# Centred rows by row tile at the head of a GLU + attention kernel, with the first weights loaded earlier

## The chip, the cores and the metric

The kernel runs on one core of one Trainium2 chip. The metric is the device time of one execution in microseconds (us). An execution also has a *span*, from the first to the last instruction in its trace; here the time is nearly always 1.7 to 2.0 us above the span.

## The reference, cut to what matters

```python
xn = _layernorm(x)                                   # (x - mean) / sqrt(var + 1e-5), 2048 rows of 512
s  = attention(xn @ wq, k_cache, v_cache) @ wo       # 32 heads, 2048 keys, Dh = 128
gate = xn @ W_gate; up = xn @ W_up                   # 512 -> 1792
h = relu(gate) * up
g = silu(h @ W_down)
return x + s * g
```

The change rests on one identity. With the centred row `xc = x - mean` and `r = 1/sqrt(var + eps) > 0`, `gate = r * (xc @ W_gate)` and `up = r * (xc @ W_up)`. ReLU passes a positive factor through, so `h @ W_down = r^2 * (h_c @ W_down)`. Gate and up can therefore run on centred rows before `r` is known, if `r^2` is applied at the SiLU.

## The kernel before

The kernel computes the GLU first and the attention after it. The GLU's gate and up use a ring of three slots of two PSUM banks (one for gate, one for up); a slot comes free when ReLU (ACT) and the product (DVE) have read it. The first 512 rows need special care, because nothing is in SBUF yet.

```python
load_x0(sp, 0); load_x0(act, 1); load_x0(sp, 2); load_x0(act, 3)   # 128 rows each
load_w(sp, Wg_sb, wg_src, sem_wg, 0); load_w(sp, Wu_sb, wu_src, sem_wu, 0)   # chunks 0 to 2
# ... later weights and rows ...

def ring_acquire():
    s = ring_cnt[0] % NSLOT
    ring_cnt[0] += 1
    _wait_all(pe, ring_tok[s])          # [ReLU token, product token] of the last user
    ring_tok[s] = []
    return s

def head_ln():
    st = ln_stats(0)
    st = ln_stats(1)
    sq01 = ln_aggr([0, 1], st)          # aggregate, then Sqrt on ACT
    st = ln_stats(2)
    c01 = ln_coef([0, 1], sq01)         # reciprocal, -mean*rstd
    n0 = ln_norm(dve, sem_ln4, 0, c01)
    n1 = ln_norm(dve, sem_ln4, 1, c01)
    head_transpose(0, n0, act, sem_xa)  # 4 PE transposes, ACT copy to xnT
    head_transpose(1, n1, act, sem_xa)
    warm_mm(3)
    # ... tiles 2 and 3 alike ...
    emit_half(0, range(HFC - 1), xt_ready[0][0:2])   # 256 columns at a time, chunks 0 and 1
    # ... then chunk 2, then emit_half(1, ...) for the other 256 columns

_wait(pe, warm_w)
warm_mm(12)                             # 512-column matmuls on zeros
head_ln()
```

After the head, `emit_gate_up` runs the remaining eleven chunks of the first 512 rows with 512-column ("full-width") matmuls. The first of these takes slot 0, so it waits until ReLU and product of chunk 0 are done.

The softmax here doesn't subtract the row's maximum and nothing guards it: scores larger than these inputs give would overflow.

## Time and profile before

| what | value |
|---|---|
| time | 1288.09 us, median of 3 (1287.98 to 1288.51) |
| span of the profiled execution | 1285.8 us |
| first useful matmul | 7.80 us |
| first full-width matmul | 13.48 us |

The page first: busy time of each engine, and the shares of the chain of work that ended last.

```profile
PE 1279.2 (99%) x11995; PEld 834.8 (65%) x11995; DVE 380.0 (30%) x682; ACT 1001.4 (78%) x1109; POOL 10.0 (1%) x21
...
PE 99%; DVE 1%; issue 0%; DMA 0%; ACT 0%
```

TensorE (PE) bounds the kernel. What is left to win is what lies in front of its first useful work. The waits of PE in the first 140 us (engine, line, what it waited for; total us, times, longest) are three:

```profile
PE ps_r L365 <- DVE warm L235: 1.2, 1, 1.2
PE ps_acc L353 <- DVE xn_sb L340: 0.7, 1, 0.7
PE ps_r L407 <- ACT xnT L359: 0.4, 1, 0.4
```

The chain of waits of the same kernel in its first 16 us, each piece with start and length in us:

```profile
0.74 2.39 DMA x_sb<-in_A_x_dram
...
3.15 1.30 DVE stats L315 x2
...
4.47 0.25 DVE mv L320 x2
...
5.40 0.17 DVE nmr L334
...
5.60 0.42 DVE xn_sb L340
...
6.16 0.40 PE ps_acc L353 x4
...
6.58 1.08 ACT xnT L359 x2
...
7.80 1.91 PE ps_r L407 x16
```

And the first full-width matmul of before, in the timeline of PE:

```profile
13.48 1.03 PE L481 MATMUL ps_r<-xnT,Wg_sb 128*128 128x512 bf16 x4
```

Two tiles go through the whole layer norm and two copies before PE can start at 7.80. From there PE is busy to the end, apart from a wait of 0.4 us near the last instruction.

### The profile page before, as it was taken

How to read it: one execution, taken by the hardware profiler on the slowest of the kernel's cores; microseconds unless marked ns; L12 is line 12 of the kernel's file. 1: busy time of each engine (PE TensorE's matmuls, PEld its weight loads, DVE VectorE, ACT ScalarE, POOL GpSimd, SP SyncE). 2: the span in 40 equal slices, each digit the busy share in tenths (PEclk: the TensorE clock that was granted, in tenths of full speed). 3: DMA queues.
4: the chain of work that ended last, by engine and by line, in shares of the span. 5: the costliest groups of instructions: out<-in, count | busy, mean ns of one | idle time of the engine just before them, and what ended most of it. 6: DMA issues, size and time to landing. Idle time of an engine off the chain costs nothing.

```text
span 1285.8 us, 26847 instructions
## 1 busy us (share of the span) xinstructions
PE 1279.2 (99%) x11995; PEld 834.8 (65%) x11995; DVE 380.0 (30%) x682; ACT 1001.4 (78%) x1109; POOL 10.0 (1%) x21
## 2 busy tenths in 40 slices
PE   9999999999999999999999999999999999999998
PEld 4444476666666666666666666666666666666665
DVE  6333311112222222222222222222222222234456
ACT  3322399998888888888888888888888888888884
POOL 2000000000000000000000000000000000000000
PEclk9999999999999999999999999999999999999999
DMA  9500123232222332232322322332223321233302
GB/s 266 111 1 1 21 36 67 57 54 40 36 51 50 71 54 50 54 71 51 54 46 37 60 47 53 55 67 55 54 51 71 55 34 38 50 67 55 50 14 74
DMA packets 238801, 71.60 MB, mean 56 GB/s; under 512 B 225632, under 2 KB 238688, under 8 KB 238688
## 3 DMA queue, kind: packets, MB, share of 16 engines
q1 hardware_dynamic: 238400, 69.63, 27.8%
q8 instruction: 96, 1.57, 0.5%
q10 hardware_dynamic: 288, 0.26, 0.1%
q14 instruction: 17, 0.14, 0.0%
HBM read 32.77 MB, written 2.10 MB: 27 GB/s over the span
## 4 chain that ended last, share of the span: by engine, by line
PE 99%; DVE 1%; issue 0%; DMA 0%; ACT 0%
PE ps_acc L722 36%; PE ps_r L625 34%; PE ps_r L558 9%; PE ps_r L579 8%; PE ps_acc L504 4%; PE ps_r L485 4%; PE ps_r L481 4%; PE ps_r L759 1%; DVE fin_tmp L767 0%; PE ps_r L407 0%; DMA x_sb<-in_A_x_dram 0%; DVE stats L315 0%; ACT xnT L359 0%; PE ps_acc L353 0%; DVE x_sb L772 0%
## 5 line engine op out<-in xcount | busy, mean ns | idle before, releaser
L635 ACT ACTIVATE PT<-ps_r 128x1024 bf16<-128x1024 f32 x1024 | 952.5, 1054 | 167.7 <-PE ps_r L625 167.7
L722 PEld LDWEIGHTS ps_acc<-V_sb,PT 128*128 128x128 bf16 x8192 | 621.1, 98 | 241.7 <-ACT PT L635 3.5
L722 PE MATMUL ps_acc<-V_sb,PT 128*128 128x129 bf16 x8192 | 776.5, 220 | 0.0
L625 PE MATMUL ps_r<-QT_sb,KT_sb 128*128 128x512 bf16 x2048 | 754.1, 379 | 0.0
L652 DVE RECIPROCAL rz_sb<-ps_acc 128x4 f32<-128x4 f32 x127 | 23.3, 183 | 729.6 <-PE ps_acc L722 729.6
L625 PEld LDWEIGHTS ps_r<-QT_sb,KT_sb 128*128 128x128 bf16 x2048 | 195.0, 98 | 1.1 <-DVE QT_sb L569 0.4
L558 PE MATMUL ps_r<-xnT,Wq_sb 128*128 128x512 bf16 x512 | 130.9, 379 | 0.0
L579 PE MATMUL ps_r<-Wo_sb,OT_store 128*128 128x512 bf16 x448 | 114.6, 379 | 0.0
L569 DVE CAST QT_sb<-ps_r 128x512 bf16<-128x512 f32 x128 | 88.5, 692 | 48.1 <-PE ps_r L558 48.1
L558 PEld LDWEIGHTS ps_r<-xnT,Wq_sb 128*128 128x128 bf16 x512 | 49.9, 97 | 60.7 <-ACT PT L635 27.1
L655 DVE TENSOR_TENSOR Onorm<-ps_acc,rz_sb 128x512 bf16<-128x512 f32 x127 | 87.8, 691 | 4.4
L579 PEld LDWEIGHTS ps_r<-Wo_sb,OT_store 128*128 128x128 bf16 x448 | 43.8, 98 | 52.9 <-ACT PT L635 0.2
L448 ACT ACTIVATE gr_sb<-ps_r 128x512 bf16<-128x512 f32 x56 | 33.3, 596 | 51.5 <-PE ps_r L481 49.9
L592 DVE TENSOR_TENSOR s_acc<-s_acc,ps_r 128x512 f32<-128x512 f32 x96 | 66.0, 687 | 17.3 <-PE ps_r L579 17.3
L485 PE MATMUL ps_r<-xnT,Wu_sb 128*128 128x512 bf16 x212 | 54.4, 379 | 0.0
L481 PE MATMUL ps_r<-xnT,Wg_sb 128*128 128x512 bf16 x212 | 54.4, 379 | 0.0
L454 DVE TENSOR_TENSOR hT<-gr_sb,ps_r 128x512 bf16<-128x512 bf16 x56 | 38.4, 686 | 46.3 <-PE ps_r L485 42.0
L504 PE MATMUL ps_acc<-Wd_sb,hT 128*128 128x512 bf16 x224 | 49.0, 379 | 0.0
L510 ACT ACTIVATE sig_sb<-ps_acc 128x512 f32<-128x512 f32 x16 | 9.6, 597 | 38.8 <-PE ps_acc L504 38.8
L504 PEld LDWEIGHTS ps_acc<-Wd_sb,hT 128*128 128x128 bf16 x224 | 21.9, 98 | 26.4
L485 PEld LDWEIGHTS ps_r<-xnT,Wu_sb 128*128 128x128 bf16 x212 | 20.7, 98 | 25.0
L481 PEld LDWEIGHTS ps_r<-xnT,Wg_sb 128*128 128x128 bf16 x212 | 20.8, 98 | 24.8
(42 smaller groups left out, 138.7 us busy)
## 6 DMA issues: line engine op xcount, KB each, us to landing
V_sb<-in_A_v_cache_dram SPq DMA_DIRECT2D x32, 512.0 KB, 4.5
Wq_sb<-in_A_wq_dram SPq DMA_DIRECT2D x32, 128.0 KB, 2.4
Wo_sb<-in_A_wo_dram SPq DMA_DIRECT2D x8, 512.0 KB, 3.9
OT_store<-Onorm SPq DMA_TRANSPOSE x127, 2.4
Wd_sb<-in_B_W_down_dram SPq DMA_DIRECT2D x1, 1792.0 KB, 13.6
x_sb<-in_A_x_dram SPq DMA_DIRECT2D x3, 512.0 KB, 10.1
out_dram<-x_sb SPq DMA_DIRECT2D x6, 256.0 KB, 2.2
Wg_sb<-in_B_W_gate_dram SPq DMA_DIRECT2D x1, 768.0 KB, 9.8
```

Source lines behind the costliest of these rows:

```text
L454: dve.tensor_tensor(hT[par][:, fc, :], gr_sb[gk][:], ps_r[:, gb + 1, :], ALU.mult)
L481: ins = pe.matmul(ps_r[:, gb, :], Wg_sb[:, c, fs], xnT[:, c, qs], start=(c == 0), stop=(c == DC - 1))
L485: ins = pe.matmul(ps_r[:, gb + 1, :], Wu_sb[:, c, fs], xnT[:, c, qs], start=(c == 0), stop=(c == DC - 1))
L504: ins = pe.matmul(ps_acc[:, jb, 0:D], hT[par][:, fc, j * 128:(j + 1) * 128], Wd_sb[:, fc, :], start=(fc == 0), stop=(fc == FC - 1))
L558: ins = pe.matmul(ps_r[:, bank, :], Wq_sb[b][:, c, :], xnT[:, c, qs], start=(c == 0), stop=(c == DC - 1))
L569: etok = sem_qpe.sig(dve.tensor_copy(QT_sb[b][:, qs], ps_r[:, bank, :]))
L579: ins = pe.matmul(ps_r[:, bank, 0:D], OT_store[g % 2][:, hh, n * 128:(n + 1) * 128], Wo_sb[g % 2][:, hh, :], start=(hh == 0), stop=(hh == ...
L592: dve.tensor_tensor(s_acc[:, n, :], s_acc[:, n, :], ps_r[:, bank, 0:D], ALU.add)
L625: ins = pe.matmul(ps_r[:, 2 * s + tt, :], KT_sb[h % 2][:, t * 128:(t + 1) * 128], QT_sb[h % 2][:, qs], start=True, stop=True)
L635: act.activation(PT[pb][:], ps_r[:, 2 * s:2 * s + 2, :], ACTF.Exp, scale=scale)
L655: dve.tensor_tensor(Onorm[ob][:], o_ap, rz_sb[:].to_broadcast([128, 4, Dh]), ALU.mult))
L722: ins = pe.matmul(o_ap, PT[pb][:, tt, j * 128:(j + 1) * 128], V_sb[vb][:, t, 0:VW], start=(t == 0 and j % 2 == 0), stop=(t == KT - 1 and j ...
```

## The change

The intent is to start PE earlier: one row tile of 128 rows at a time, with nothing but statistics and a subtraction in front of it, and with the first weights ahead of x tiles 2 and 3, since they would otherwise be late for the earlier start. The normalised rows, which attention still needs, are made later on POOL and transposed by DMA. The diff, cut to its core:

```diff
                 load_x0(sp, 0)
                 load_x0(act, 1)
+                load_w(sp, Wg_sb, wg_src, sem_wg, 0)
+                load_w(act, Wu_sb, wu_src, sem_wu, 0)
                 load_x0(sp, 2)
                 load_x0(act, 3)
-                load_w(sp, Wg_sb, wg_src, sem_wg, 0)
-                load_w(sp, Wu_sb, wu_src, sem_wu, 0)
@@ ... @@
+                def head_center(n):
+                    atok = ln_aggr([n], ln_stats(n))
+                    _wait(dve, atok)
+                    return sem_ln4.sig(
+                        dve.tensor_scalar(xc_sb[:, n, :], x_sb[:, n, :], mv[:, n, 0:1], None, op0=ALU.subtract))
@@ head_ln: the body shown above is replaced @@
+                    ctok = {0: head_transpose(0, head_center(0))}
+                    warm_mm(2)
+                    for n in range(4):
+                        if n + 1 < 4:
+                            ntok = head_center(n + 1)
+                        _wait(pe, ctok[n])
+                        head_tile(n, 0)           # 4 gate + 4 up matmuls of 128 columns
+                        if n + 1 < 4:
+                            ctok[n + 1] = head_transpose(n + 1, ntok)
+                        for fc in range(1, HFC):
+                            head_tile(n, fc)
@@ emit_down, first 512 rows @@
-                            act.activation(sig_sb[jb][:], ps_acc[:, jb, 0:D], ACTF.Tanh, scale=0.5))
+                            act.activation(sig_sb[jb][:], ps_acc[:, jb, 0:D], ACTF.Tanh,
+                                           scale=r2h[:, j, 0:1] if Q == 0 else 0.5))
@@ ... cut: for Q == 0, sig = (tanh + 1) * r2 and then g = sig * ps_acc, in two DVE instructions @@
@@ ... @@
-                warm_mm(12)
+                warm_mm(10)
@@ ... cut: square root, coefficients and r2 for rows 0 to 511 move behind the other rows; POOL normalises them;
@@ gate/up of the first 512 rows reads xcT; attention waits for the transposes of rows 0 to 511 @@
```

More of the change, by code (lines that the diff above doesn't have):

```diff
@@ L141, in bass_recurrent_scan__mha_block_cached__glu_gated_reglu__prompt_kernel @@
         xn_sb = SB_([128, NT, D], BF16, "xn_sb")
+        xc_sb = SB_([128, 4, D], BF16, "xc_sb")
+        xcT = SB_([128, DC, NQ], BF16, "xcT")
+        r2 = SB_([128, 4, 1], F32, "r2")
+        r2h = SB_([128, 4, 1], F32, "r2h")
         stats = SB_([128, NT, 6], F32, "stats")
@@ L320, in ln_aggr, with ln_sqrt @@
                         atok = sem_ln2.sig(dve.bn_aggr(mv[:, n, :], stats[:, n, :]))
+                    return atok
+                def ln_sqrt(ns, atok):
                     a, b_ = ns[0], ns[-1] + 1
                     _wait(act, atok)
-                    if a == 0:
-                        _wait(act, warm_tok)
                     return sem_sq.sig(
@@ L343, in _, with head_transpose @@
                 xt_ready = {Q: [] for Q in range(QB)}
-                def head_transpose(n, ntok, eng, sem):
+                def head_center(n):
[3 more added lines that the diff above has]
+                        dve.tensor_scalar(xc_sb[:, n, :], x_sb[:, n, :], mv[:, n, 0:1], None, op0=ALU.subtract))
+                def head_transpose(n, ntok):
                     tp_ps = acc_bf[n % 2]
@@ L353, in head_transpose @@
                         ins = pe.transpose(tp_ps[:, c * 128:(c + 1) * 128],
-                                           xn_sb[:, n, c * 128:(c + 1) * 128], ident[:])
+                                           xc_sb[:, n, c * 128:(c + 1) * 128], ident[:])
                     ptok = sem_tp.sig(ins)
                     src = tp_ps[:, 0:DC * 128].rearrange("p (c q) -> p c q", c=DC)
-                    _wait(eng, ptok)
-                    copy = act.copy if eng is act else dve.tensor_copy
-                    ctok = sem.sig(copy(xnT[:, :, n * 128:(n + 1) * 128], src))
-                    xt_ready[0].append(ctok)
-                    acc_free[n % 2] = ctok
+                    _wait(act, ptok)
+                    acc_free[n % 2] = sem_xa.sig(act.copy(xcT[:, :, n * 128:(n + 1) * 128], src))
+                    return acc_free[n % 2]
                 def warm_mm(k):
@@ L367, in head_ln @@
                 def head_ln():
-                    st = ln_stats(0)
-                    st = ln_stats(1)
-                    sq01 = ln_aggr([0, 1], st)
-                    st = ln_stats(2)
-                    c01 = ln_coef([0, 1], sq01)
-                    n0 = ln_norm(dve, sem_ln4, 0, c01)
-                    n1 = ln_norm(dve, sem_ln4, 1, c01)
-                    head_transpose(0, n0, act, sem_xa)
-                    head_transpose(1, n1, act, sem_xa)
-                    warm_mm(3)
-                    st = ln_stats(3)
@@ L379, in head_ln @@
-                    sq23 = ln_aggr([2, 3], st)
-                    emit_half(0, range(HFC - 1), xt_ready[0][0:2])
-                    c23 = ln_coef([2, 3], sq23)
-                    n2 = ln_norm(dve, sem_ln4, 2, c23)
-                    n3 = ln_norm(dve, sem_ln4, 3, c23)
-                    head_transpose(2, n2, act, sem_xa)
-                    head_transpose(3, n3, dve, sem_xt)
-                    emit_half(0, range(HFC - 1, HFC), [])
-                    emit_half(1, range(HFC), xt_ready[0][2:4])
@@ L389, in _ @@
-                half_slots = []
-                def emit_half(k, fcs, toks):
-                    hs = slice(k * 256, (k + 1) * 256)
-                    for fc in fcs:
-                        fs = slice(fc * 128, (fc + 1) * 128)
-                        if k == 0:
-                            if fc == 0:
-                                pe.wait_ge(sem_wg[0].h, 16)
-                            half_slots.append(ring_acquire())
-                        if fc == 0:
-                            _wait_all(pe, toks)
-                        s = half_slots[fc]
-                        for i, W in enumerate((Wg_sb, Wu_sb)):
-                            if k == 0 and fc == 0 and i == 1:
-                                pe.wait_ge(sem_wu[0].h, 16)
-                            ins = None
-                            for c in range(DC):
-                                ins = pe.matmul(ps_r[:, 2 * s + i, hs], W[:, c, fs], xnT[:, c, hs],
-                                                start=(c == 0), stop=(c == DC - 1))
-                            if k == 1:
-                                half_tok[(fc, i)] = (sem_gate if i == 0 else sem_gu).sig(ins)
+                    ctok = {0: head_transpose(0, head_center(0))}
@@ new lines, in head_ln, with head_tile @@
+                    warm_mm(2)
[8 more added lines that the diff above has]
+                            head_tile(n, fc)
+                half_slots = []
+                def head_tile(n, fc):
+                    hs = slice(n * 128, (n + 1) * 128)
+                    fs = slice(fc * 128, (fc + 1) * 128)
+                    if n == 0:
+                        half_slots.append(ring_acquire())
+                    s = half_slots[fc]
+                    for i, (W, sems) in enumerate(((Wg_sb, sem_wg), (Wu_sb, sem_wu))):
+                        if n == 0 and fc == 0:
+                            pe.wait_ge(sems[0].h, 16)
+                        ins = None
+                        for c in range(DC):
+                            ins = pe.matmul(ps_r[:, 2 * s + i, hs], W[:, c, fs], xcT[:, c, hs],
+                                            start=(c == 0), stop=(c == DC - 1))
+                        if n == 3:
+                            half_tok[(fc, i)] = (sem_gate if i == 0 else sem_gu).sig(ins)
@@ L412, in _, with ln_finish @@
                 half_tok = {}
                 ln_hold = {}
+                def ln_finish(Q):
+                    ns, sqtok = ln_hold.pop("sq")
+                    ctok = ln_coef(ns, sqtok)
+                    for n in ns:
+                        ntok = ln_norm(pool, sem_nm, n, ctok)
+                        _wait(sp, ntok)
+                        xt_tok = sem_xq[Q].sig(
+                            sp.dma_start_transpose(xnT[:, :, n * 128:(n + 1) * 128], xn_sb[:, n, :]))
+                    xt_ready[Q] = [xt_tok]
+                    return ctok
@@ L416, in ln_task @@
                 def ln_task(i):
                     if i < 4 * (QB - 1):
-                        n = 4 + i
-                        ln_hold["st"] = ln_stats(n)
-                    if i % 4 == 3 and 4 + i < NT:
-                        Q = 1 + i // 4
-                        ns = list(range(4 * Q, 4 * Q + 4))
-                        ln_hold["sq"] = (ns, ln_aggr(ns, ln_hold["st"]))
-                    elif "sq" in ln_hold:
-                        ns, sqtok = ln_hold.pop("sq")
-                        ctok = ln_coef(ns, sqtok)
-                        for n in ns:
-                            ntok = ln_norm(pool, sem_nm, n, ctok)
-                            _wait(sp, ntok)
-                            Q = n // 4
-                            xt_tok = sem_xq[Q].sig(
-                                sp.dma_start_transpose(xnT[:, :, n * 128:(n + 1) * 128], xn_sb[:, n, :]))
-                        xt_ready[Q] = [xt_tok]
-                        if Q == QB - 1:
-                            issue_first()
+                        ln_hold["st"] = ln_stats(4 + i)
@@ new lines, in ln_task @@
+                        if i % 4 == 3:
+                            ns = list(range(i + 1, i + 5))
+                            ln_hold["sq"] = (ns, ln_sqrt(ns, ln_aggr(ns, ln_hold["st"])))
+                        elif i >= 4 and i % 4 == 0:
+                            ln_finish(i // 4)
+                    elif i == 4 * (QB - 1):
+                        ln_finish(QB - 1)
+                        issue_first()
+                        ns = list(range(4))
+                        ln_hold["sq"] = (ns, ln_sqrt(ns, sem_ln2.cur()))
+                    elif i == 4 * (QB - 1) + 1:
+                        ctok = ln_finish(0)
+                        _wait(dve, ctok)
+                        rtok = sem_ln3.sig(dve.tensor_tensor(r2[:], rstd[:, 0:4, :], rstd[:, 0:4, :], ALU.mult))
+                        _wait(dve, rtok)
+                        ln_hold["r2"] = sem_ln3.sig(
+                            dve.tensor_scalar(r2h[:], r2[:], 0.5, None, op0=ALU.mult))
@@ L474, in emit_gate_up @@
                             _wait_all(pe, xt_ready[Q])
+                        xT, xs = (xcT, slice(0, NQ)) if Q == 0 else (xnT, qs)
                         if Q == 0 and fc in FCS:
@@ L480, in emit_gate_up @@
                         for c in range(DC):
-                            ins = pe.matmul(ps_r[:, gb, :], Wg_sb[:, c, fs], xnT[:, c, qs],
+                            ins = pe.matmul(ps_r[:, gb, :], Wg_sb[:, c, fs], xT[:, c, xs],
                                             start=(c == 0), stop=(c == DC - 1))
@@ L484, in emit_gate_up @@
                         for c in range(DC):
-                            ins = pe.matmul(ps_r[:, gb + 1, :], Wu_sb[:, c, fs], xnT[:, c, qs],
+                            ins = pe.matmul(ps_r[:, gb + 1, :], Wu_sb[:, c, fs], xT[:, c, xs],
                                             start=(c == 0), stop=(c == DC - 1))
@@ L508, in emit_down @@
                         _wait(act, sig_free[jb])
+                        if Q == 0 and j == 0:
+                            _wait(act, ln_hold["r2"])
                         stok = sem_sig.sig(
-                            act.activation(sig_sb[jb][:], ps_acc[:, jb, 0:D], ACTF.Tanh, scale=0.5))
+                            act.activation(sig_sb[jb][:], ps_acc[:, jb, 0:D], ACTF.Tanh,
+                                           scale=r2h[:, j, 0:1] if Q == 0 else 0.5))
                         _wait(dve, stok)
-                        gtok = sem_g.sig(
-                            dve.scalar_tensor_tensor(g_sb[:, n, :], sig_sb[jb][:], 1.0, ps_acc[:, jb, 0:D],
-                                                     op0=ALU.add, op1=ALU.mult))
+                        if Q == 0:
+                            ttok = sem_g.sig(
+                                dve.tensor_scalar(sig_sb[jb][:], sig_sb[jb][:], 1.0, r2[:, j, 0:1],
+                                                  op0=ALU.add, op1=ALU.mult))
+                            _wait(dve, ttok)
+                            gtok = sem_g.sig(
+                                dve.tensor_tensor(g_sb[:, n, :], sig_sb[jb][:], ps_acc[:, jb, 0:D], ALU.mult))
+                        else:
+                            gtok = sem_g.sig(
+                                dve.scalar_tensor_tensor(g_sb[:, n, :], sig_sb[jb][:], 1.0, ps_acc[:, jb, 0:D],
+                                                         op0=ALU.add, op1=ALU.mult))
                         y_bank_free[jb] = gtok
@@ L518, in emit_down @@
                     hT_free[par] = ytok
-                assert DC == 4 and FC >= 4 * (QB - 1) + 1
+                assert DC == 4 and QB >= 2 and FC >= 4 * (QB - 1) + 2
                 _wait(pe, warm_w)
-                warm_mm(12)
+                warm_mm(10)
                 head_ln()
@@ L555, in emit_qp @@
                     _wait(pe, wq_tok(h))
+                    if h == 0 and Q == 0:
+                        _wait_all(pe, xt_ready[0])
                     ins = None
```

## The prediction

> **What bounds the kernel.** TensorE. The page gives PE 99% of a 1285.8 us span, and the chain of waits is 99% PE. The waits of PE over the first 140 us come to three: 1.2 us (start), 0.7 us (first normalised tile) and 0.4 us (first copied transpose). So all that this change can win lies before 13.5 us, where the first full-width gate/up matmul starts (timeline); about 140 us of GLU work and 1140 us of attention behind it keep PE busy and do not change. Total useless PE time is only the first 7.8 us, 0.6% of the span: over 2% is out of reach.
>
> **The head before** (chain of waits): x tile lands 3.13; two statistics (1.30), aggregate, square root, reciprocal, coefficient, normalise end 6.02; transposes 6.16; two ACT copies 6.58 to 7.66; first useful matmul 7.80. Then 48 matmuls of 256 columns (0.108 us each) and 8 transposes (0.056 each) keep PE busy to 13.48.
>
> **Removed:** from the first chain, the second statistics, square root, reciprocal, coefficient and second copy. New chain: x 3.13, statistics to 3.83, aggregate 4.0, centring (the normalise took 0.41) to 4.5. The ten warm-up matmuls still occupy PE until about 4.85, so transposes run 4.85 to 5.1, the copy (0.54) ends near 5.85, first useful matmul near 6.0: 1.8 us earlier.
>
> **Weights:** before, the first up weights landed near 7.7 (issue 2.12, 5.6 to landing). Now they are issued about 1 us earlier, on two queues, ahead of two x tiles; DMA moves about 365 GB/s here (stretches of 1 us), so 256 KB + 768 KB from about 2.2 us should land by 5.4 to 6.0. The Trainium skill, "DMA: Bandwidth & Descriptors", section "Queues, rings and completion order", says engines alternate between queue rows, so x tiles 2 and 3 should land only slightly later (about 6.1), and they are needed after 5.9 and 7.2. This may cost some tenths.
>
> **Added:** 96 matmuls of 128 columns in place of 48 of 256. The attention matmuls of 129 columns, each with its own weights, took 0.057 us each (0.23 per four), so 5.5 us instead of 5.2; head from 6.0 to about 12.15.
>
> **New wait:** the first full-width matmul needs bank slot 0, i.e. ReLU (0.60) and product (0.69) of chunk 0. Before, 2.15 us of PE work followed its last gate group; now only about 1.15 us, while ReLU + product + hand-over take about 1.6. PE stalls about 0.5 us; full-width work starts near 12.65, 0.8 us earlier than 13.48. Later weights (landed 11.3 before) should arrive in time.
>
> **Moved off path:** the normalisation of rows 0 to 511 goes to POOL (0.77 per tile) and DMA transposes, needed only at 141 us. In the first down projection the extra DVE product (estimate 0.4 to 0.7 us per tile) fits: PE takes 3.02 us per tile, tanh + product took 1.3. Tables: the late square root still precedes the tanh load, so no additional table load.
>
> **Prediction:** 1288.09 - 0.8 = 1287.3 us, 1286.2 to 1288.4 eight times in ten. Faster by over 2%: 0.01; within 2%: 0.98; slower by over 2%: 0.01.
>
> **Right or wrong shows in:** first useful matmul in the timeline (6.0 against 7.80); the group of 128-column matmuls, 96 at about 0.057 apart; a wait of PE on DVE's product of about 0.5 us before the first full-width matmul; its start (12.65 against 13.48); everything afterwards shifted by the same amount, the first down projection at 12.1 us unchanged, no PE wait at 141 us.
>
> **What would make it wrong:** weights or x tile 2 landing after 6.5 us, so PE stalls in the head; 128-column matmuls running slower than 0.057; the slot stall passing on to the next two slots; run-to-run spread (0.5 us) as large as the gain.

## The result, and the profile after

| | runs | median us | range us |
|---|---|---|---|
| before | 6 | 1288.03 | 1287.91 to 1288.51 |
| after | 6 | 1287.09 | 1286.87 to 1287.75 |

The ratio is 0.9993 (95% interval 0.998 to 1.0006). Ratios are the mean time of one kernel's fast runs over that of the other's of the same rounds, so not quite the ratio of the medians. The difference of the means is 0.88 us, where 0.8 had been predicted.

The profile does not look like this gain. The trace is of the slowest of the six runs: its span is 1286.0 us (the six spans run from 1285.0 to 1286.0), and its first full-width matmul starts at 13.63 us, later than the 13.48 of before. The page of the changed kernel, busy time by engine:

```profile
PE 1279.3 (99%) x12040; PEld 835.4 (65%) x12040; DVE 382.0 (30%) x685; ACT 1001.7 (78%) x1109; POOL 13.2 (1%) x25
```

The waits of PE in the first 150 us of the changed kernel, same columns as above:

```profile
PE ps_r L374 <- DVE warm L239: 1.2, 1, 1.2
PE ps_r L402 <- DMA Wu_sb<-in_B_W_up_dram: 0.5, 1, 0.5
PE ps_r L488 <- ACT gr_sb L454: 0.4, 1, 0.4
PE ps_r L402 <- ACT xcT L369: 0.2, 1, 0.2
```

And its chain of waits in the first 16 us:

```profile
1.18 6.01 DMA Wu_sb<-in_B_W_up_dram
...
7.23 0.40 PE ps_r L402 x4
7.63 0.22 PE ps_acc L364 x4
...
10.98 1.13 PE ps_r L402 x20
...
12.13 1.09 ACT gr_sb L454 x2
13.23 0.40 issue
13.63 1.02 PE ps_r L488 x4
```

The layer norm is gone from the chain. In its place stands the load of the first up weights, 6.01 us from issue to landing, and a new wait of PE between the last 128-column matmul (its last group starts at 12.82, and a group takes 0.22, so PE is through at 13.04) and the first full-width one at 13.63: 0.59 us. The 128-column matmuls themselves go as predicted: eight (a gate and an up group) every 0.446 us, 0.056 us each.

One check makes the rest simple. In every trace in which the record of the first full-width matmul is not missing, it starts 1272.3 to 1272.4 us before the end of the span: 1285.8 - 13.48 before, 1286.0 - 13.63 after. Whatever happens to the time happens in the first 14 us. The moved normalisation, the extra DVE instruction and the later table load cost nothing: no PE wait on them exists, and the first down projection takes 12.25 us in both traces.

### The profile page after: what moved, and what is told of

It reads as the page before. It is cut to its first block, busy times and chain, and to the rows that moved or that the text cites. A ratio compares the mean times of both kernels' runs of the same rounds, so it can differ in the third digit from the quotient of the medians.

```text
span 1286.0 us, 26948 instructions
## 1 busy us (share of the span) xinstructions
PE 1279.3 (99%) x12040; PEld 835.4 (65%) x12040; DVE 382.0 (30%) x685; ACT 1001.7 (78%) x1109; POOL 13.2 (1%) x25
## 4 chain that ended last, share of the span: by engine, by line
PE 98%; DVE 1%; DMA 0%; issue 0%; ACT 0%; ACTq 0%
PE ps_acc L742 36%; PE ps_r L645 34%; PE ps_r L578 9%; PE ps_r L599 8%; PE ps_acc L511 4%; PE ps_r L488 4%; PE ps_r L492 4%; PE ps_r L779 1%; DMA Wu_sb<-in_B_W_up_dram 0%; DVE fin_tmp L787 0%; PE ps_r L402 0%; ACT gr_sb L454 0%; DVE x_sb L792 0%; PE ps_acc L364 0%; DVE Onorm L696 0%
## 5 line engine op out<-in xcount | busy, mean ns | idle before, releaser
L492 PE MATMUL ps_r<-xnT,Wu_sb 128*128 128x512 bf16 x168 | 43.1, 379 | 0.0
L488 PE MATMUL ps_r<-xnT,Wg_sb 128*128 128x512 bf16 x168 | 43.1, 379 | 0.0
L488 PEld LDWEIGHTS ps_r<-xnT,Wg_sb 128*128 128x128 bf16 x168 | 16.4, 98 | 19.8
L492 PEld LDWEIGHTS ps_r<-xnT,Wu_sb 128*128 128x128 bf16 x168 | 16.4, 98 | 19.8
```

Of the source, the lines that this page charges most:

```text
L488: ins = pe.matmul(ps_r[:, gb, :], Wg_sb[:, c, fs], xT[:, c, xs], start=(c == 0), stop=(c == DC - 1))
L492: ins = pe.matmul(ps_r[:, gb + 1, :], Wu_sb[:, c, fs], xT[:, c, xs], start=(c == 0), stop=(c == DC - 1))
```

## The experiments

Times are means of the five runs, and the last column is the difference from the mean of the nine runs of before in the same call (1288.04, 1288.09 and 1288.00).

| run | chip call | mean us | range us | against before |
|---|---|---|---|---|
| repeat1 | 1 | 1287.32 | 1287.06 to 1287.85 | -0.72 |
| order_only | 1 | 1290.91 | 1290.72 to 1291.19 | +2.87 |
| centre_only | 1 | 1288.60 | 1288.29 to 1288.99 | +0.56 |
| gates_first | 1 | 1287.68 | 1286.94 to 1288.11 | -0.36 |
| split_wait | 2 | 1286.73 | 1286.60 to 1286.93 | -1.36 |
| warm8 | 2 | 1287.44 | 1287.05 to 1287.81 | -0.65 |
| split_warm8 | 2 | 1286.89 | 1286.49 to 1287.27 | -1.20 |
| halves | 2 | 1287.77 | 1287.08 to 1288.71 | -0.32 |
| repeat2 | 3 | 1287.62 | 1287.09 to 1288.12 | -0.38 |
| split_gates | 3 | 1286.64 | 1286.46 to 1286.99 | -1.36 |
| one_queue | 3 | 1287.62 | 1287.56 to 1287.82 | -0.38 |
| before_split | 3 | 1288.25 | 1287.83 to 1288.55 | +0.25 |

The theory: the gain is the earlier start of PE in the head, made possible only by centring *and* the load order together, and what eats part of it is the landing of the up weights (which varies) and the wait for slot 0 (which is constant). Rivals stand in each expectation.

### The change again: repeat1 and repeat2

No edit.

> The changed kernel, unaltered. In its profile the first up weights landed at 7.19 us and the span was 1286.0, the longest of its six runs (1285.0 to 1286.0). Theory A: the spread comes from when these weights land; in an execution with a span near 1285.1 they land about 0.9 us earlier, near 6.3, the first up matmul starts near 6.5 instead of 7.23 and full-width work near 12.7 to 12.9 instead of 13.63. Rival B: the spread comes from somewhere behind the head; then full-width work starts near 13.6 again whatever the span is. Time: 0.6 to 1.0 us below before.

> The changed kernel again, for a third profile and as the yardstick of this call: 1286.9 to 1287.4 us. Full-width work starts 1272.3 to 1272.4 us before the end of the span, as in all profiles so far, so anything the span differs by must be visible before that start.

The chain of waits of repeat1, with a span of 1285.4 us:

```profile
1.19 4.35 PE ps_r L374 x10
5.53 0.24 PE ps_acc L364 x4
...
5.79 0.59 ACT xcT L369
...
6.43 0.62 PE ps_r L402 x8
...
13.05 1.02 PE ps_r L488 x4
```

The waits of PE in repeat2, with a span of 1286.3 us (the line that differs):

```profile
PE ps_r L402 <- DMA Wu_sb<-in_B_W_up_dram: 0.9, 1, 0.9
```

The same program has three heads in three executions. The up weights landed at 6.2 (1.18 + 5.0, repeat1), 7.2 (the first trace) and 7.6 us (repeat2), and PE waited for them 0, 0.5 and 0.9 us. Full-width work started at 13.05, 13.63 and 13.99 us, and the spans were 1285.4, 1286.0 and 1286.3. So in these three traces the difference comes from the landing of these weights: theory A holds, except that repeat1's start at 13.05 is later than I had written (12.7 to 12.9), because the warm-up matmuls held the transposes (see the warm-up and the half rate below). What makes the landing vary was not tested and stays open. The time of repeat1 was as expected; the mean of repeat2, 1287.62, lies above the 1286.9 to 1287.4 that I had written. Over all sixteen runs of the change the mean gain is 0.67 us ((6 x 0.88 + 5 x 0.72 + 5 x 0.38) / 16).

### One part alone: order_only and centre_only

order_only is the kernel before with the new loads, centre_only the change with the old ones:

```diff
 # order_only: before.py                        # centre_only: after.py with the reverse of it
                 load_x0(sp, 0)
                 load_x0(act, 1)
+                load_w(sp, Wg_sb, wg_src, sem_wg, 0)
+                load_w(act, Wu_sb, wu_src, sem_wu, 0)
                 load_x0(sp, 2)
                 load_x0(act, 3)
-                load_w(sp, Wg_sb, wg_src, sem_wg, 0)
-                load_w(sp, Wu_sb, wu_src, sem_wu, 0)
```

> Before, with only the new order of loads (first gate and up weights ahead of x tiles 2 and 3, up weights on ACT's queue). Theory: this alone costs time, because the old chain of the first two tiles has the statistics of tile 2 in the middle of DVE's order, and tile 2 now lands near 7 us instead of before 4.7: first useful matmul near 9.5 to 10.5 instead of 7.80, full-width work 1.5 to 2.5 us later, 1289.5 to 1290.5 us. Rival: the load order is what wins the time, and the centred rows are incidental; then it is at or below 1287.5.

> The changed kernel with the old order of loads. Theory: the centred chain is ready at the same time (copy near 6.3), but the first up weights land near 7.7 as before, so the first up matmul starts near 7.75, 0.5 us later than in the profiled run of the change, and full-width work near 14.1: about 0.5 us slower than before, 1288.5 us. Rival: centring alone wins the 0.9 us whatever the loads do, 1287.1.

Each part alone costs time: +2.87 and +0.56 us, where both together win 0.67. Waits of PE in centre_only:

```profile
PE ps_r L402 <- DMA Wu_sb<-in_B_W_up_dram: 0.7, 1, 0.7
PE ps_r L402 <- DMA Wg_sb<-in_B_W_gate_dram: 0.4, 1, 0.4
```

With the old order the early start runs into both weights. The time was as expected (1288.60 against 1288.5); the profiled execution, the longest of the five, had the up weights later (8.4 us against 7.7) and full-width work later (14.84 against 14.1) than I had written. In order_only the direction was as expected, and the first useful matmul at 9.91 us lies in the expected range, but the loss was larger than the 1.5 to 2.5 us I had written: full-width work started at 16.82 us, 3.3 later than in the profile of before (about 3.0 later than in a usual execution of before, see the half rate below). The statistics of tile 2, which stand in the middle of DVE's order, waited for their x tile until 6.73 us, against 4.64 before (timeline of DVE):

```profile
6.73 0.69 DVE L315 BATCH_NORM_STATS2 stats<-x_sb 128x6 f32<-128x512 bf16 x1 [1.70 <-DMA x_sb<-in_A_x_dram]
```

The timeline of PE (start, length, operation) and the busy time in one stretch (after the DVE, ACT and POOL columns: granted clock, DMA share, GB/s) show what followed:

```profile
8.28 0.63 PE L353 MATMUL ps_acc<-ident,xn_sb 128*128 128x128 bf16 x8 [2.15 <-DVE xn_sb L340]
...
9.91 1.01 PE L407 MATMUL ps_r<-xnT,Wg_sb 128*128 128x256 bf16 x4
10.72 1.06 PE L407 MATMUL ps_r<-xnT,Wu_sb 128*128 128x256 bf16 x4
11.57 1.03 PE L407 MATMUL ps_r<-xnT,Wg_sb 128*128 128x256 bf16 x4
12.43 0.62 PE L407 MATMUL ps_r<-xnT,Wu_sb 128*128 128x256 bf16 x4
```

```profile
9.00:13.00 4.00, 4.00 (x22) 2.40 (x21) 1.36 (x7) 0.97 (x3) 0.00 (x0) 0.57 1.08 361
```

PE stood idle 2.15 us waiting for the normalised rows, and afterwards its matmuls went at half rate (groups of four 256-column matmuls 0.81 to 0.86 us apart until 12.4, against 0.43 in the trace of before), at a granted clock of 0.57. That a gap of 2.15 us came before is seen, but the eight transposes right behind it still ran at full rate (8.28 to 8.74); whether the gap caused the half rate was not tested.

### Late up weights: gates_first, one_queue, split_gates

gates_first runs the three gate groups of tile 0 ahead of its three up groups; one_queue issues the up weights on SP's queue.

```diff
 # gates_first (split_gates adds the split wait of the next section, and transposes tile 1 after the first gate group)
+                        if n == 0:
+                            for fc in range(HFC):
+                                head_tile(0, fc, (0,))      # gate only
+                            ctok[1] = head_transpose(1, ntok)
+                            for fc in range(HFC):
+                                head_tile(0, fc, (1,))      # up only
+                            continue
 # one_queue
-                load_w(act, Wu_sb, wu_src, sem_wu, 0)
+                load_w(sp, Wu_sb, wu_src, sem_wu, 0)
```

> The changed kernel, with the three gate groups of tile 0 ahead of its three up groups, so that up weights are needed 0.44 us later. Theory A (late up weights stall PE by up to 0.5 us in some executions, and none in others): the stall shrinks by up to 0.44 us, mean 0.1 to 0.4 us below the change, and the spread over runs is smaller. Rival (PE waits for something else by then, such as x tile 2): no gain.

> The changed kernel with the first up weights issued on SP's queue behind the gate weights, not on ACT's. Theory: they are issued 0.47 us later, and nothing but two x tiles and the gate weights lie ahead of them; they land 6.7 to 7.4 us, and PE stalls for them in most executions: 0.2 to 0.5 us slower than the change (1287.3 to 1287.7 us). Rival: the DMA engines are the limit and not the issue, so the landing and the time stay where they are.

> The split slot wait, and in tile 0 the order: first gate group, transposes of tile 1, two gate groups, three up groups. Theory: up weights are needed 0.44 us later, so an execution with late up weights loses at most some 0.1 us instead of up to 0.5, and (unlike in the run with all three gates first) 1.1 us of PE work lie behind the transposes, so that the copy of tile 1 costs nothing: 1286.4 to 1286.7 us, at or below the split wait alone (1286.68), with a smaller spread. Rival (clock ramp and x tile 2 are what is left): same as the split wait alone within 0.1 us.

gates_first missed: 0.36 us slower in mean than the change in the same call. Its edit brought a wait of its own. Only three up groups lie behind the transposes of tile 1, and the copy takes longer: the next tile started 0.84 us after the first up group, where the same twelve matmuls take 0.67 in split_gates. In its trace PE also started late, at 6.74. So it decided nothing about the weights.

one_queue missed too. I had expected 0.2 to 0.5 us more than the change; both have a mean of 1287.62. The up weights landed at about 6.7 us (issue 1.68, 5.0 to landing), inside the 6.2 to 7.6 of the two-queue version, and no PE wait on them is in its trace. Its five runs lie within 0.26 us, against 1.03 for repeat2. So no gain of the second queue was seen. That it has none is not shown: this trace started late, with the first gate matmul at 6.74 and the first up matmul at 6.97, so that weights landing at 6.7 could cost nothing, where they would have cost a PE that started at 6.33; and the change itself was at its slowest (-0.38 us against before, -0.72 and -0.88 in the others). The one queue seems to land the weights more regularly, but one trace does not show that.

split_gates has the same mean gain as the split wait alone (-1.36 both). In its trace the up weights landed at about 6.3, before they were needed, so it could not show what the reordering is worth when they are late. That stays open.

### The wait for slot 0: split_wait and before_split

The wait between the last 128-column and the first full-width matmul was put down to ACT's ReLU by the profile. But the DVE product of chunk 0 ran from 12.84 to 13.53 in that trace, and the matmul started at 13.63 (timeline of DVE in the changed kernel):

```profile
12.84 0.69 DVE L460 TENSOR_TENSOR hT<-gr_sb,ps_r 128x512 bf16<-128x512 bf16 x1 [3.27 <-PE ps_r L402]
```

The gate bank is free after the ReLU, and only the up bank needs the product. The edit makes each group wait for its own bank alone; it was checked to be free of races.

```diff
+                def ring_acquire_split():
+                    s = ring_cnt[0] % NSLOT
+                    ring_cnt[0] += 1
+                    rtok, htok = ring_tok[s]
+                    _wait(pe, rtok)
+                    ring_tok[s] = []
+                    return s, htok
@@ emit_gate_up @@
-                        s = ring_acquire()
+                        s, up_free = ring_acquire_split()
@@ @@
                         gtok = sem_gate.sig(ins)
+                        _wait(pe, up_free)
```

> The changed kernel; full-width gate matmuls wait only for the ReLU that frees the gate bank of their slot, and the up matmuls for the product that frees the up bank. Theory: in the repeated look at the change PE stood idle from 12.47 to 13.05 us, 0.58 us, for ReLU and product of chunk 0; ReLU had ended by 12.15, so this wait goes and 0.5 to 0.6 us are won against the change: 1286.6 us, full-width work directly behind the last 128-column matmul. Rival: the wait only moves to the up matmuls or to the next slots; gain under 0.2 us.

> Before, with the split slot wait alone. Theory: before has 2.15 us of PE work behind the last gate group of the first chunk and no slot wait in its profile, so nothing is won: 1288.0 us within 0.15. Rival: the split wait wins something everywhere (later slots, too): 1287.5 us or less.

In the waits of PE of split_wait only two lines are left for the first 150 us:

```profile
PE ps_r L382 <- DVE warm L239: 1.2, 1, 1.2
PE ps_r L410 <- ACT xcT L377: 0.2, 1, 0.2
```

The timeline of PE in split_wait; the record of the first of the four full-width gate matmuls is missing from the trace, so the first line of them shows three:

```profile
12.26 0.39 PE L410 MATMUL ps_r<-xcT,Wu_sb 128*128 128x128 bf16 x4
12.69 0.81 PE L496 MATMUL ps_r<-xcT,Wg_sb 128*128 128x512 bf16 x3
13.34 1.03 PE L501 MATMUL ps_r<-xcT,Wu_sb 128*128 128x512 bf16 x4
```

From 12.26 to 12.69 are 0.22 us for the last group and 0.21 for the missing matmul: no gap. The mean is 1286.73, all five runs (1286.60 to 1286.93) below the fastest of the nine runs of before (1287.85). The cleanest measure of the wait is the pair warm8 and split_warm8 of the same call, which differ in this edit alone: 1287.44 - 1286.89 = 0.55 us, against 0.5 to 0.6 expected. Their ranges overlap (1287.05 to 1287.81 and 1286.49 to 1287.27), so the size is rough; the traces show the wait itself, 0.59 us in warm8 and none in split_warm8. In before, the same edit won nothing (+0.25 us in mean, its range overlapping that of before, and 0.1 above the range that I had written). So the slot wait was brought in by the change, and because the gate group needs only the ReLU and PE did not wait for it, it was the product that PE had waited for, not the ReLU that the profile names.

### The warm-up: warm8 and split_warm8

```diff
-                    warm_mm(2)       # behind the transposes of tile 0
+                    warm_mm(4)
@@ @@
-                warm_mm(10)
+                warm_mm(8)
```

> The changed kernel with two of the ten warm-up matmuls moved behind the first transposes (8 and 4 instead of 10 and 2). Theory: the first centred tile is ready at 4.60 us but the transposes start at 5.26 to 5.43, held by the warm-up at half rate (0.427 us per matmul). With 8 they start near 4.7, and the first copy ends near 5.7. Then the first gate weights (landing near 6.0) and up weights (6.2 to 7.2) are the limit: gain 0 to 0.4 us in mean, with a DMA wait of PE in every profile. Rival: PE's warm-up is the only limit, weights never matter; gain 0.6 us.

> Both of the two edits before. Theory: they act at different places, so gains add: 0.5 to 0.9 us below the change, 1286.2 to 1286.6 us. It should then be the fastest of all.

Both missed: warm8 is 1287.44, within the range of the change and without the PE wait for weights that I had expected in every profile, and split_warm8 is not faster than split_wait but 0.16 us slower in mean, with overlapping ranges. The timeline of PE in warm8:

```profile
4.85 0.58 PE L364 MATMUL ps_acc<-ident,xc_sb 128*128 128x128 bf16 x4
5.23 1.78 PE L374 MATMUL ps_r<-warm 128*128 128x512 bf16 x4
6.84 0.39 PE L402 MATMUL ps_r<-xcT,Wg_sb 128*128 128x128 bf16 x4
```

The transposes did start earlier, 4.85 instead of 5.26. But the four filling matmuls behind them then held PE until 6.84, because PE was still at half rate. Moving the warm-up moved its cost. Neither of my two theories had this term. In split_warm8 the half rate ended sooner: its four filling matmuls held PE only until 6.40, and then PE waited 0.46 us for the up weights. So in that trace the weights were the limit, as my theory had it.

### Where the half rate comes in

In the trace of before, which I had used for the prediction, the weight loads of the warm-up go from 0.43 us apart to about 0.22 at 4.16 us (timeline of PE's weight loads):

```profile
3.73 0.15 PEld L365 LDWEIGHTS ps_r<-warm 128*128 128x128 bf16 x1 [0.27 <-issue]
4.16 0.79 PEld L365 LDWEIGHTS ps_r<-warm 128*128 128x128 bf16 x4 [0.28 <-issue]
```

In the trace of after, they are still 0.42 apart there:

```profile
3.73 0.15 PEld L374 LDWEIGHTS ps_r<-warm 128*128 128x128 bf16 x1 [0.27 <-issue]
4.16 0.15 PEld L374 LDWEIGHTS ps_r<-warm 128*128 128x128 bf16 x1 [0.28 <-issue]
4.58 0.15 PEld L374 LDWEIGHTS ps_r<-warm 128*128 128x128 bf16 x1 [0.28 <-issue]
```

The change does not touch these instructions. before_split, whose head is that of before, shows that the same head can also run later: its first useful matmul came at 8.32 instead of 7.80, and full-width work at 14.00 instead of 13.48. Its statistics of the first tiles, its transposes, and the matmuls behind them:

```profile
3.48 1.29 DVE L323 BATCH_NORM_STATS2 stats<-x_sb 128x6 f32<-128x512 bf16 x2 [2.35 <-DMA x_sb<-in_A_x_dram]
6.48 0.84 PE L361 MATMUL ps_acc<-ident,xn_sb 128*128 128x128 bf16 x8
7.16 0.81 PE L373 MATMUL ps_r<-warm 128*128 128x512 bf16 x3
```

Two things were late in it. The first x tile: its statistics started at 3.48 us instead of 3.15, so that the first tile was normalised at 6.33 instead of 6.02 and transposed from 6.48 instead of 6.16. And the half rate lasted longer: the twelve warm-up matmuls took 5.30 us instead of 4.25, which by itself held up nothing, because the first normalised tile came later still; but the eight transposes took 0.68 us (6.48 to 7.16) instead of 0.46. Together, these 0.32 and 0.22 us make up the 0.52 within 0.02.

The Trainium skill, "TensorE: Matmul & The Clock Gate", section "Part 1: The HAM clock gate", says that the array starts at half rate and that the moment of the change varies by half a microsecond either way from run to run, since its time window runs freely. These traces agree that the moment varies, but over a wider range: it lay at about 4.2 us in before and at about 7.0 in before_split (its transposes start 0.106 us apart until 6.97 and 0.056 apart from 7.05 on), with the same head; in warm8 it lay after 6.5.

So the profile of before was a lucky one, in both: no other of the fourteen traces has its first statistics as early as 3.15 us (3.18 to 3.70), and in none of them did the half rate end as early as 4.2. Its span of 1285.8 us lies below every one of the 27 spans of before measured beside the experiments (1285.9 to 1286.5, mean 1286.16). With 1272.33 us behind the first full-width matmul, that matmul starts at about 13.8 us in a usual execution of before (an estimate from these two numbers), not at 13.48.

### Two halves instead of four row tiles: halves

```diff
-                    hs = slice(n * 128, (n + 1) * 128)
+                    hs = slice(n * 256, (n + 1) * 256)
 # head_ln: centre and transpose tiles 0 and 1, chunks 0 and 1 of half 0, transpose tiles 2 and 3,
 # chunk 2 of half 0, then half 1; tile 3 is copied on DVE, as before
```

> The changed kernel with centring and the new load order, but the first chunks in two halves of 256 columns as before instead of four row tiles of 128. Theory: it starts about 0.6 us later (two centred tiles and two copies needed, near 7.0), but takes 5.6 us instead of 6.0, and has 2.15 us of PE work behind the first chunk's last gate group, so no slot wait: full-width work at 12.7 to 12.9, 0.2 to 0.4 us better than the change (1286.8 us). Rival: the row tiles are what wins; then it is 0.3 us or more slower than the change.

Its trace starts at 6.99 us as expected and has no slot wait, but PE waited 0.6 us in two pieces for centred tiles: 0.28 for tile 1, which DVE centres after tile 0, and 0.32 for tile 3, whose turn on DVE came late because x tile 2, now behind the weights, kept DVE waiting until 6.81. Its span was 1285.5; the mean span of the five runs, 1285.48, equals that of the change (1285.55 over sixteen), while the mean time is 1287.77, since three of the five times lie 2.5 us or more above their span instead of 1.7 to 2.0. Whether halves are slower than row tiles is open. That they are no faster is as far as it goes, and my expectation of 1286.8 was wrong.

## Why the prediction was right

Predicted and measured, in us; the change has three traces.

| step | predicted | first trace, repeat1, repeat2 |
|---|---|---|
| first gate matmul | 6.0 | 6.33, 6.43, 6.33 |
| up weights landed | 5.4 to 6.0 | 7.2, 6.2, 7.6 |
| one 128-column matmul | 0.057 | 0.056 in all |
| last 128-column matmul done | 12.15 | 13.04, 12.47, 13.41 |
| wait for slot 0 | 0.5 | 0.59, 0.58, 0.58 |
| first full-width matmul | 12.65 | 13.63, 13.05, 13.99 |
| time | -0.8 | -0.88, -0.72, -0.38 (means) |

- **Right: the ceiling and the place.** PE is busy from its first full-width matmul on (apart from 0.4 us near the end, as before), and all that the change did lies before the first full-width matmul. The 1272.3 us behind it did not change.
- **Right: the price of narrow matmuls.** 96 matmuls of 128 columns at 0.056 us, read off the attention matmuls of 129 columns.
- **Right: the slot wait.** 0.5 us were predicted from the order of the groups and the lengths of ReLU and product; 0.58 was seen, and taking it away won 0.55.
- **Right: what moved off the path cost nothing.** The tanh with a scale per row took 0.69 us instead of 0.60, and the added DVE product 0.49 us (estimate 0.4 to 0.7), while PE needs 3.02 us per tile.
- **Mis-sized: "The ten warm-up matmuls still occupy PE until about 4.85".** They held the transposes until 5.26, 5.37 and 5.26 us. I had taken the early end of the half rate in one trace for a property of the kernel. This is 0.4 us. (The "x 3.13" of the prediction was early, too: the first statistics started at 3.30, 3.56 and 3.18 us. But the first tile was centred by 4.60, 4.86 and 4.47, before the warm-up let PE go, so this cost nothing here.)
- **Mis-sized: the up weights "should land by 5.4 to 6.0".** They landed at 6.2 to 7.6, and PE waited 0, 0.5 and 0.9 us. I had named this as what could go wrong and put it at "some tenths".
- **Mis-sized, without a cost here: x tile 2 "about 6.1".** Its statistics, which waited for it, started at 7.06, 6.56 and 6.85 us. In the change, x tiles 2 and 3 each stand behind weights in their own queue, so alternation between the queues could not bring them ahead of these. That the two queue rows alternate, as the skill's page says, fits one_queue, where the x tiles on ACT's queue, with no weights among them, took a median of 2.8 us to land instead of 4.3 in the first trace of the change. The tile was centred by 8.36 us in the first trace and 7.86 in repeat1, and PE took it up at 9.03 and 8.46, so nothing waited.
- **Why the total came out all the same.** These two terms make the first full-width matmul 0.4 to 1.3 us later than predicted. But the 13.48 us that I subtracted from was itself early, with its early x tile and its early full rate: a usual execution of before has about 13.8. The difference of the mean spans, 1286.16 - 1285.55 = 0.61 us, and the mean gain of 0.67 us are what is left. The mechanism was right, but that the total came out within 0.2 us is partly luck: two errors met whose effects on the difference have opposite signs.

The fastest version found keeps the change and lets each bank of a slot be waited for separately: 1286.73 us in mean (split_wait), 1.36 us below before, twice the mean gain of the change alone. split_gates reached the same gain on another chip.

## What to carry to other kernels

A rearrangement that starts an engine earlier must be costed to where the old schedule takes over again: here the shorter tail of the head turned a hidden chain of ReLU and product into a wait of 0.58 us, and waiting per bank took it away. Two parts of a change can each cost time and win together, as the early start and the early weights did. When the effect is a few tenths of a microsecond, one trace is one draw: look at the spans of all runs to see whether the trace you read from is a typical one before you subtract from it.

## What the Trainium skill lacked or had wrong

- "TensorE: Matmul & The Clock Gate", section "Back-to-back issue gap", gives about 81 ns per matmul for a sustained stream of weight load and matmul pairs at 128 columns, and about 131 ns at 512. Here 96 matmuls of 128 columns, each with its own weight load, ran at 56 ns each (four in 0.223 us), and 512-column ones at 216 ns (four in 0.86 us). The formula of the same section for a single matmul, N/2.4 + 2.5 ns (55.8 and 215.8 ns), fits the sustained stream.
- The same page, section "Part 4: PE-mode transpose", gives about 275 to 390 ns for a 128x128 transpose and says that the full clock does not engage for it. Here four in a row took 0.22 us (56 ns from start to start) once PE was warm, and 0.42 us at half rate (one_queue, 5.43 to 5.85). So transposes did run at the full rate. How long one takes alone was not measured.
- No page that I read says that the granted clock in the profile can read 1.00 while the matmuls go at half rate. Between 1.20 and 4.00 us the changed kernel's row reads 1.00 although the weight loads of its 512-column matmuls are 0.43 us apart; only the later half rate of order_only showed, as 0.57. The stretch of the changed kernel, same columns as above:

```profile
1.20:4.00 2.80, 2.80 (x7) 1.03 (x8) 0.69 (x1) 1.49 (x2) 0.48 (x4) 1.00 0.69 192
```

- "DMA: Bandwidth & Descriptors", section "Queues, rings and completion order", describes how the queue rows share the DMA engines but gives no spread of landing times. The same load of 384 KB, issued at the same 1.18 us on ACT's queue, took 5.0, 6.0 and 6.4 us to land in three traces of the change, and 4.4 in that of split_wait (issued at 1.16).
- "TensorE: Matmul & The Clock Gate", section "Part 1: The HAM clock gate": the half microsecond either way quoted above was too narrow here. In the same head the full rate came at about 4.2 us (before) and about 7.0 us (before_split), with the first warm-up matmul at 1.19 in both.
